# Local attention and Fourier mixing in one kernel: batch 0's three-point sums move to VectorE, crossbar transposes become 768 columns wide, and the planner counts eight DMA places

## The chip, the cores and the metric

The kernel runs on one core of a Trainium2 chip. The metric is the device time of one execution in microseconds (us), as a median over several runs. The core has TensorE (PE, with its weight loads PEld), VectorE (DVE), ScalarE (ACT), GpSimd (POOL) and SyncE (SP, which here only issues transfers). Sixteen DMA engines move the data.

## The reference

Four batches, eight heads, 768 positions, 64 numbers a head. First comes attention with a linear distance penalty, in which a query sees the 95 keys before it, itself, and the first eight keys of the sequence. Then follows a Fourier layer with a feed-forward block (model width 512, hidden width 2048).

```python
scores = scale * np.matmul(q, k.transpose(0, 1, 3, 2))
bias = -slopes[:, None, None] * dist[None, :, :]
scores = np.where(keep, scores + bias, -1e9)        # keep: local band or first 8 keys
x = np.matmul(softmax(scores), v)                   # heads side by side: (B, S, 512)
X = np.fft.fft(np.fft.fft(x, axis=1), axis=2)
u = x + np.real(X)
un = (u - mean(u)) / np.sqrt(var(u) + 1e-6)
out = u + np.maximum(un @ w_ch1, 0.0) @ w_ch2
```

## The kernel before, in words

**Attention.** For each batch and each pair of heads (hp 0 to 3), q and k are loaded as float32, cast to float16 (`cast_qk` L382 for batches 0 and 1, `cast_direct` L400 for 2 and 3) and transposed. Batches 0 and 1 use PE for that (`trans` L515, tile pt, copied out by DVE at L533 or ACT at L537). Batches 2 and 3 (`b >= FB`) use the DMA crossbar (`trans_dma` L499, issued by SP at L506): four transfers for each head pair, each of 64 partitions by 768 columns. `score` (L542) multiplies key tiles of 128 by the queries of the same and the next tile. In batches 0 and 1 the distance penalty is added by a further product; in batches 2 and 3 ACT's exponential goes to a buffer `er`, and DVE multiplies it with a mask `mk` (L592). `v_global` and `glob` treat the first eight keys, `av` (L665) multiplies with v and normalizes into X[b], and `bounce` (L720) writes X[b] to DRAM (xd) and reads it back in another order (xr), to be added later. Batch 0's bounce is issued by SP, the others' by ACT.

**Fourier layer.** The transform over 768 positions is split into a step of 6 and a step of 128, the one over 512 columns into a step of 4 and a step of 128. The small steps are sums on DVE, the large ones products on PE. For batches 1 to 3, `fold_s` (L741, stages f1 to f4) makes the two-point and three-point sums, and `fold_d` (L841, stages g1 and g2) the four-point sums over the columns. For batch 0 (`b < DB`, DB = 1), `fold_3` (L797) makes only the two-point and four-point sums; the three-point sum is left to PE, which adds three products with different tables in PSUM. `y_unit` (L878) makes these products, py: for batch 0 with tables t1 and t1x (five further blocks, 480 KB, loaded at L1290 into a buffer of the ring hT), for the others with t1 alone. `mirror` (L922) reverses parts on POOL, and `u_unit` (L961) makes the second product (pu), adds xr and normalizes.

**Feed-forward.** Each batch has three chunks of 256 rows, c = 0 to 11. `nt_unit` (L1052) transposes a chunk: on PE for c below 7 (ptu, copied out by DVE or ACT), and by two crossbar transfers of 128 by 512 from c = 7 (`nt_dma` L1043). `ph_unit` (L1081) makes the hidden layer, eight groups of eight products; `pg_unit` (L1104) and, from chunk 8, `pg_units` make the output. The weights come as eight transfers of 512 KB issued by POOL (L1345, L1350); their first one waits for POOL's cast of the last k of batch 1, whose staging shares their buffers. After the last one SP issues a small transfer (hold, L1359), and only behind this gate are the loads of batch 2 issued.

**Order.** The class `Plan` (L18) decides while the program is built in which order instructions stand. It keeps a clock for each engine, adds assumed costs, and picks the next step by time, then by a rank (a lower one first). `LAND` gives assumed landing times for the first transfers. Each engine runs its instructions in that fixed order, and SP and ACT issue their transfers in it too. A transfer issued by SP or ACT takes one of eight completion semaphores in turn, and it waits until the transfer that had this semaphore before it has landed; the plan before does not count that.

Of the kernel before, what the change touches and what calls it, by code (L numbers as in the profile page):

```python
# [14 lines left out]
P = 128  # L15


class Plan:  # L18
# [8 lines left out]
    LAND = {("xw", 0, 0): 36.0, ("xw", 0, 1): 37.6, ("xr", 0): 43.3, ("ld", 4, 2): 50.1, ("ld", 5, 2): 55.5, ("ld", 6, 2): 60.9,  # L27
            ("ld", 7, 2): 66.4, ("w1", 0): 45.8, ("w1", 1): 50.6, ("w1", 2): 54.3, ("w1", 3): 57.9, ("w2", 0): 61.6, ("w2", 1): 65.2, ("w2", 2): 68.1, ("w2", 3): 70.7}
    LAT = {"ACT": 0.14, "DVE": 0.12, "POOL": 0.08}

    def __init__(self):
        self.t = {"PE": 0.0, "ACT": 0.0, "DVE": 0.0, "POOL": 0.0, "SP": 0.7, "DMA": 1.9, "DMA2": 0.0}
        self.tok = {}
        self.ready = []
        self.pending = []
        self.rings = {}
        self.left = {}
        self.n = 0

# [23 lines left out]
    def later(self, ways, needs=(), after=0.0, outs=(), uses=(), ring=None, lat=0.0, dma=0.0, then=None, rank=1):  # L63

        self.n += 1
        self.pending.append((self.n, ways, list(needs), after, outs, uses, ring, lat, dma, then, rank))
        self.promote()
# [11 lines left out]
    def first(self):  # L79

        best = None
        for i, (ready, p) in enumerate(self.ready):
            c = (min(max(self.t[w[0]], r) for w, r in zip(p[1], ready)), p[10], ready[0], p[0], i)
            if best is None or c < best:
                best = c
        return best

    def emit(self, place):
        ready, (_, ways, needs, after, outs, uses, ring, lat, dma, then, _) = self.ready.pop(place)
# [12 lines left out]
        for u in uses:  # L102
            self.used(u, end + lat)
        if ring is not None:
# [5 lines left out]
    def pe(self, us, after=0.0):  # L110
# [6 lines left out]
    LOOK = 10  # L117

# [60 lines left out]
def kernel(  # L179
# [24 lines left out]
    DB = 1  # L204
# [78 lines left out]
    NBUF = {"hT": 3, "qk": 2, "qs": 3, "qkT": 4, "er": 2, "eg": 1, "x": 1, "xr": 1, "zy": 1, "eA": 1,  # L283
# [43 lines left out]
    def load(b, hp, which):  # L327
# [3 lines left out]
        if b >= FB:  # L331
            srcs = [(0, q), (1, k)] if which == "qk" else [(2, v)]
            for w, src in srcs:
                i = 1 + HP + 3 * (n - FB * HP) + w

                def run(src=src, i=i, w=w):
                    t = stage[("t", n, w)] = buf("qs", i, [P, 2 * NS, Dh], FP32, 1)
                    if w < 2:
# [5 lines left out]
                pl.later([("SP", 0.55 if w < 2 else 1.1, run)], free("qs", i) + gate, 0.0, [("ld", n, w)], lat=1.7, dma=2.67)  # L344
# [55 lines left out]
    def cast_direct(b, hp, w, i):  # L400
        n = HP * b + hp

        def cast(on):
            if n not in qk16:
                qk16[n] = buf("qk", n, [P, 2, 2, NP, 2, Dh], FP16, 1)
            for t in range(2):
                copy_on(on, qk16[n][:, t, w], stage[("t", n, w)].rearrange("p (h i t) d -> p t i h d", h=2, t=2)[:, t])
        pl.later([("ACT", act(768), lambda: cast("ACT")), ("POOL", 1.6, lambda: cast("POOL"))],
# [7 lines left out]
    def cast_v0(b, hp):  # L416
        n = HP * b + hp

        def cast():
            V0[n] = buf("er", n, [P, NP, 2, 2, Dh], FP16, 1)  # L420
            nc.gpsimd.tensor_copy(V0[n].rearrange("p n t h d -> p (n t) h d"),
                                  stage[("t", n, 2)].rearrange("p (h n) (t d) -> p h (n t) d", h=2, t=2).rearrange("p h j d -> p j h d"))
        pl.later([("POOL", 0.87, cast)], [("ld", n, 2)] + free("er", n), 0.0, [("vc", n)], [("free",) + vat(n)], rank=b)

    def v_place(b, hp):
        n = HP * b + hp

        def run(start, ring):
# [14 lines left out]
            pl.used(("free", "er", n), e)  # L443
# [43 lines left out]

    def kg_copies(b, hp):
        n = HP * b + hp
        for s in range(2):  # L490
            def cp(s=s):
# [3 lines left out]
                    TT[n][64 * s:64 * s + 64, 1, 0:P].rearrange("p (t m) -> p t m", t=2)[:, :, 0:NG // 2])  # L495
# [3 lines left out]
    def trans_dma(b, hp):  # L499
        n = HP * b + hp  # L500

        def xb(a, t):
            if n not in TT:
                TT[n] = buf("qkT", n, [P, 2, S], FP16, 6)
            o = TT[n].rearrange("p w (i a t m) -> p a t (w i) m", a=2, t=2, m=64)[:, a, t]
            nc.sync.dma_start_transpose(o, qk16[n][64 * a:64 * a + 64, t].rearrange("p w i h d -> p (w i h d)"))  # L506
        at = [(a, t) for a in range(2) for t in range(2)]
        for x, (a, t) in enumerate(at):
            pl.later([("SP", 1.3, lambda a=a, t=t: xb(a, t))],
                     ([("qk", n, 0), ("qk", n, 1)] + free("qkT", n)) if x == 0 else [("xb", n, x - 1)], 0.0,  # L510
                     [("xb", n, x)], lat=0.0, dma=0.01)
        pl.later([("SP", 0.0, lambda: None)], [("xb", n, 3)], 0.0, [("qkT", n)], [("free", "qk", n)], lat=2.2, dma=0.5)
# [28 lines left out]

    def score(b, hp, g):  # L542
        n = HP * b + hp
        idx = 2 * HP + 3 * (n - 2 * HP) + g

        def run(start, ring):
            pa = bank(ring, f"sc_{n}_{g}")
            w0, w1_ = ((256, CO), (CO, CO), (256, P))[g]
            tiles = ((2 * g, 0, w0), (2 * g + 1, 256, w1_))
            if b < 2:  # L550
# [10 lines left out]
            for i, c0, cw in tiles:  # L561
                for s in range(2):
                    lo = 64 * s
                    nc.tensor.matmul(pa[:, s, c0:c0 + cw], TT[n][lo:lo + 64, 1, i * P:(i + 1) * P],  # L564
                                     TT[n][lo:lo + 64, 0, i * P:i * P + cw], start=(b > 1), stop=True,
                                     skip_group_check=(b < 2))
            e = pl.pe(0.24 if b > 1 else 0.66, start)
# [17 lines left out]
            if b < 2:  # L585
# [17 lines left out]
        ATT.append(([("qkT", n)] + ([("sid", hp), ("c", "dist")] if b < 2 else []), BANKS(b), run))  # L603
# [29 lines left out]
    def glob(b, halves):  # L633
# [4 lines left out]
        def run(start, ring):  # L638
            pg = bank(ring, f"pgl_{b}_{halves[0]}")
            for half in halves:  # L640
                for i in range(2):
                    hp = 2 * half + i
                    nc.tensor.matmul(pg[32 * half:32 * half + 32, 0, :], kG[b % 2][:, hp, :],
                                     TT[HP * b + hp][:, 0, 256:S], start=(i == 0), stop=(i == 1),
                                     tile_position=(0, 32 * half))
            e = pl.pe(mm_us(512, 2 * len(halves)), start)
# [14 lines left out]
    XT = [("x", 0), ("hT", 4), ("x", 1), ("x", 2)]  # L661
# [3 lines left out]
    def av(b, part, jp):  # L665
# [8 lines left out]
        def run(start, ring):  # L674
# [31 lines left out]
            def norm():  # L706
                if b not in X:
                    X[b] = buf(XT[b][0], XT[b][1], [P, NS, Dm], FP16, 4 if b else 5)
# [11 lines left out]
    def bounce(b):  # L720
# [3 lines left out]
        for n, (c0, c1) in enumerate(parts):  # L724
            def wr(n=n, c0=c0, c1=c1):
# [3 lines left out]
                for t in range(2):  # L729
# [3 lines left out]
                     lat=1.7, dma=2.4 if b else 2.6)  # L733
# [6 lines left out]

    def fold_s(b):  # L741

        parts = ((0, 256), (256, 128), (384, 128)) if b == 0 else ((0, 512),)
# [732 lines left out]
```

## Time and profile before

| what | value |
|---|---|
| median of 9 runs | 269.54 us (269.02 to 271.84) |
| the profiled execution | 270.51 us, of which its span (first to last instruction) 268.7 us |
| instructions in the span | 6248, of which 2540 products on PE |
| granted clock of PE | 1.00 |
| moved by DMA | 42.03 MB, 75743 packets, 32834 of them under 512 bytes |
| HBM | 31.92 MB read, 9.44 MB written |

The page gives busy times of the engines, and the trace can be asked for groups of instructions, waits, the chain of work that ended last, and tables by stage. A product's listed length includes its way through the array, and products overlap; so what one costs in a row of many is read from the distance between starts. A wait is told with its releaser: `PE ph L1091 <- ACT hT L1097` means that PE stood idle before a ph product of line 1091 until ACT's instruction of line 1097 was done. SPq and ACTq are issues of transfers, in which the engine itself does nothing else.

### The profile page before, as it was taken

To read this page: it belongs to the slowest core of one execution; us is meant where nothing else is said; L and a number is where in the kernel's file an instruction comes from. 1 tells how busy PE (TensorE), PEld (TensorE's weight loads), DVE (VectorE), ACT (ScalarE), POOL (GpSimd) and SP (SyncE) were. 2 spreads that over 40 slices of the span, in tenths; PEclk is the share of its full clock that TensorE was granted. 3 is DMA by queue.
4 is the path that set the end of the run, shared out by engine and by line. 5 is a ranking of instruction groups with operands and counts; after the bars stand their busy time and mean duration, and the time that the engine had idled before them with its cause. 6 is when DMAs were issued, how large, how long until landed. Compare 5 with 4: busy or idle time off the path is not lost.

```text
span 268.7 us, 6248 instructions
## 1 busy us (share of the span) xinstructions
PE 255.0 (95%) x2540; PEld 181.2 (67%) x2540; DVE 171.8 (64%) x349; ACT 151.1 (56%) x263; POOL 61.0 (23%) x127
## 2 busy tenths in 40 slices
PE   7799899999999899999999799999999999999994
PEld 3454558577855776676675356759777668888883
DVE  4566873833399475861559957878998645525473
ACT  1479693987536737994891254896443345444300
POOL 1442298142010152321200307101100511010000
PEclk9999999999999999999999999999999999999999
DMA  7999969999689985997899896402072241311122
GB/s 211 290 294 307 280 158 256 217 215 213 130 157 255 279 161 133 207 192 130 209 156 174 181 315 150 106 2 41 0 168 109 59 92 47 81 40 41 39 82 78
DMA packets 75743, 42.03 MB, mean 156 GB/s; under 512 B 32834, under 2 KB 71746, under 8 KB 75714
## 3 DMA queue, kind: packets, MB, share of 16 engines
q1 hardware_dynamic: 68658, 32.71, 52.0%
q0 software_dynamic: 4224, 4.19, 9.5%
q10 hardware_dynamic: 2832, 4.72, 6.8%
q8 instruction: 20, 0.33, 0.5%
q14 instruction: 9, 0.07, 0.1%
HBM read 31.92 MB, written 9.44 MB: 154 GB/s over the span
## 4 chain that ended last, share of the span: by engine, by line
PE 66%; DMA 20%; DVE 5%; POOL 2%; SPq 2%; ACT 2%; issue 1%; ACTq 0%; POOLq 0%
PE ph L1091 26%; PE pg L1114 12%; DMA w<-in_moe_w_ch_dram 10%; DMA qs<-in_q_dram 5%; PE pgD L1195 5%; PE sc L564 4%; PE py L892 4%; PE pgA L1195 4%; PE pav L691 3%; DMA u<-in_v_dram 3%; PE pu L972 3%; DMA qs<-in_v_dram 2%; PE sc L559 2%; PE pt L527 1%; SPq L372 1%; POOL ww L940 1%
## 5 line engine op out<-in xcount | busy, mean ns | idle before, releaser
L1091 PE MATMUL ph<-unT,w 128*128 128x256 f16 x768 | 94.1, 273 | 2.7 <-ACT hT L1097 1.6
L1091 PEld LDWEIGHTS <-w 128*128 128x128 f16 x768 | 72.6, 98 | 17.1 <-issue 6.1
L1097 ACT ACTIVATE hT<-ph 128x512 f16<-128x512 f32 x78 | 46.2, 596 | 41.7 <-PE ph L1091 41.6
L1114 PE MATMUL pg<-w,hT 128*128 128x512 f16 x256 | 60.7, 379 | 0.0
L1114 PEld LDWEIGHTS <-hT 128*128 128x128 f16 x256 | 24.2, 98 | 23.4 <-issue 0.6
L587 ACT ACTIVATE ex<-sc 128x992 f16<-128x992 f32 (+2 forms) x24 | 20.8, 926 | 8.2 <-PE sc L564 8.2
L584 ACT ACTIVATE er<-sc 128x992 f16<-128x992 f32 (+2 forms) x24 | 21.6, 923 | 3.9 <-PE sc L564 3.1
L376 ACT ACTIVATE qk<-qs 128x384 f16<-128x384 f32 (+1 forms) x29 | 13.8, 526 | 15.1 <-DMA qs<-in_q_dram 5.1
L1098 DVE TENSOR_SCALAR hT<-ph 128x512 f16<-128x512 f32 x18 | 12.4, 691 | 11.6 <-PE ph L1091 11.6
L1123 DVE SCALAR_TENSOR_TENSOR u<-pg,sm,u 128x512 f32<-128x512 f32 x16 | 12.0, 748 | 12.1 <-PE pg L1114 12.1
L466 POOL CAST v<-qs 128x768 f16<-128x768 f32 x8 | 7.0, 879 | 52.6 <-DMA qs<-in_v_dram 52.6
L564 PE MATMUL sc<-qkT 64*128 64x256 f16 (+1 forms) x192 | 17.0, 262 | 1.4 <-ACT er L584 1.4
L691 PE MATMUL pav<-v,ex 128*128 128x65 f16 x352 | 16.3, 193 | 1.0 <-DVE x L711 0.7
L599 DVE TENSOR_TENSOR ex<-er,mk 128x992 f16<-128x992 f16 (+2 forms) x24 | 14.8, 624 | 3.6 <-ACT er L584 3.5
L691 PEld LDWEIGHTS <-ex 128*128 128x128 f16 x352 | 15.2, 97 | 2.4 <-DVE x L711 0.9
L564 PEld LDWEIGHTS <-qkT 64*128 64x128 f16 x192 | 5.9, 94 | 15.6 <-issue 14.0
L1038 POOL TENSOR_SCALAR sm<-sm 128x2 f32<-128x2 f32 x12 | 2.3, 193 | 57.1 <-ACT un L1031 57.0
L907 ACT ACTIVATE zy<-py 128x1024 f16<-128x1024 f32 (+1 forms) x12 | 10.0, 845 | 9.1 <-PE py L892 8.1
L940 POOL COPY ww<-zy 128x512 f16<-128x512 f16 x16 | 9.9, 650 | 22.9 <-PE py L892 20.8
L1031 ACT ACTIVATE un<-un 128x512 f16<-128x512 f16 x24 | 14.9, 624 | 0.3 <-PE ptu L1063 0.3
L991 DVE SCALAR_TENSOR_TENSOR u<-pu,xr 128x512 f32<-128x512 f32 x18 | 11.7, 688 | 5.0 <-PE pu L972 3.2
L1195 PEld LDWEIGHTS <-hT 128*128 128x128 f16 x128 | 12.5, 98 | 1.6
(129 smaller groups left out, 381.4 us busy)
## 6 DMA issues: line engine op xcount, KB each, us to landing
out_dram<-u SPq DMA_DIRECT2D x24, 256.0 KB, 2.4
w<-in_moe_w_ch_dram POOLq DMA_DIRECT2D x8, 512.0 KB, 19.4
qs<-in_q_dram SPq DMA_DIRECT2D x9, 384.0 KB, 6.1
qs<-in_k_dram SPq DMA_DIRECT2D x9, 384.0 KB, 6.5
qs<-in_v_dram SPq DMA_DIRECT2D x16, 192.0 KB, 4.7
xr<-xd ACTq DMA_DIRECT2D x3, 768.0 KB, 5.3
u<-in_v_dram SPq DMA_DIRECT2D x5, 384.0 KB, 7.1
w<-in_q_dram SPq DMA_DIRECT2D x4, 384.0 KB, 7.0
```

The costliest lines, as they stand in the source:

```text
L376: A(d, s, AF.Copy)
L564: nc.tensor.matmul(pa[:, s, c0:c0 + cw], TT[n][lo:lo + 64, 1, i * P:(i + 1) * P], TT[n][lo:lo + 64, 0, i * P:i * P + cw], start=(b > 1), s ...
L584: A(mine(), cut(pa), AF.Exp, 0.0, 0.125)
L587: A(cut(expst[hp][:, :, g * 512:g * 512 + (384 if g == 2 else 512)]), cut(pa), AF.Exp, 0.0, 0.125)
L599: VT(o, mine(), m, op=ALU.mult)
L691: nc.tensor.matmul(po[:, jj, hh * 65:(hh + 1) * 65], lhsT, v16[b % 2][:, i, h, 0:65], start=(jp == 0 and a == 0), stop=(a == len(ops) - 1) ...
L940: nc.gpsimd.tensor_copy(rev[:, n], T[("y", b)][:, n, :, :, ::-1])
L1031: A(x, x, AF.Square, accum_out=MV[c][:, a, 2:3])
L1091: nc.tensor.matmul(ph[:, a * CH:(a + 1) * CH], W1[0][:, d, jb * P:(jb + 1) * P], UNT[c][:, d, :], start=(d == 0), stop=(d == ND - 1))
L1097: pl.later([("ACT", act(512), lambda: A(dst, ph, AF.Relu)), ("DVE", dve(512), lambda: V.tensor_scalar_max(dst, ph, 0.0))], [], e, [("h", c ...
L1114: nc.tensor.matmul(pg, HT[c][:, jb, t * P:(t + 1) * P], W2[0][:, jb, :], start=(jb == 0), stop=(jb == NJ - 1))
L1195: nc.tensor.matmul(o, lhs(j), rhs(j), start=(first and j == 0), stop=(j == NK - 1), skip_group_check=True)
```

## The change

It has these parts:

1. DB goes from 1 to 0: batch 0 too uses `fold_s` and `fold_d`. Its columns are taken in two parts of 256, and these steps get rank -1 with a head start of 0.8 us in the plan. py of batch 0 has 24 products in place of 60, and t1x is not loaded.
2. `trans_dma` issues two transfers of 128 partitions by 768 columns for each head pair, one for q and one for k, each after its own cast. For that, k of batches 2 and 3 is loaded like v, in two transfers of 256-byte runs in place of one of 512-byte runs; and the products read q by strided patterns (`tile_of`).
3. Chunks from c = 3 on (before: from 7) are transposed by the crossbar, with one transfer of 128 by 1024. The layout of unT changes, so that a ph product reads two runs of 128 columns.
4. A whole cast of 768 columns replaces two of 384 in batches 2 and 3.
5. `cast_v0` gets buffers of its own (v0) in place of two of the ring er.
6. In batches 2 and 3 score products of 240 columns become 256 wide, and the products of `glob` go from one of 512 columns to two of 256.
7. The plan counts eight places for transfers, adds 0.1 us where PE goes between 64-row and 128-row products, and has other landing times.

```diff
-    LAND = {("xw", 0, 0): 36.0, ("xw", 0, 1): 37.6, ("xr", 0): 43.3, ...
+    LAND = {("xw", 0, 0): 34.3, ("xw", 0, 1): 36.3, ("xr", 0): 40.7, ...
...
+        self.lanes = [0.0] * 8
...
+            if p[11]:
+                ready = [max(r, self.lanes[p[11] - 1]) for r in ready]
+            c = (min(max(self.t[w[0]], r) for w, r in zip(p[1], ready)) - self.AHEAD * (p[10] < 0), p[10], ready[0], p[0], i)
...
+        for _ in range(nd):
+            self.lanes.append(max(end + lat, self.t[eng] + 2.2, *[self.LAND.get(o, 0.0) for o in outs]))
+            self.lanes.pop(0)
...
-    DB = 1
+    DB = 0
...
-                    if w < 2:
+                    if w < 1:
                         run_dma(t.rearrange("p (m t) d -> p m (t d)", t=2), src, b, h0)
                         return
...
+    def tile_of(n, lo, w, i, nb=1):
+
+        x = TT[n][lo:lo + 64, w]
+        if n < FB * HP or w:
+            return x[:, i * P:i * P + P].rearrange("p (t m) -> p t m", t=2)
+        if nb == 1:
+            return x.rearrange("p (i t a m) -> p i a t m", t=2, a=2, m=64)[:, i // 2, i % 2]
+        if i % 2 == 0:
+            return x.rearrange("p (i t a m) -> p i a t m", t=2, a=2, m=64)[:, i // 2]
+        o = (i // 2) * 256 + 64
+        return x[:, o:o + 384].rearrange("p (y q m) -> p y q m", y=2, m=64)[:, :, 0:3:2]
...
-        def xb(a, t):
+        def xb(w):
             if n not in TT:
                 TT[n] = buf("qkT", n, [P, 2, S], FP16, 6)
-            o = TT[n].rearrange("p w (i a t m) -> p a t (w i) m", a=2, t=2, m=64)[:, a, t]
-            nc.sync.dma_start_transpose(o, qk16[n][64 * a:64 * a + 64, t].rearrange("p w i h d -> p (w i h d)"))
...
+            nc.sync.dma_start_transpose(TT[n][:, w].rearrange("p (j x) -> p j x", x=P),
+                                        qk16[n][:, w].rearrange("p n t h d -> p (n t h d)"))
...
+    def RF(b):
+        return 1 if b else -1
...
-        parts = ((0, 256), (256, 128), (384, 128)) if b == 0 else ((0, 512),)
+        parts = ((0, 256), (256, 256)) if b == 0 else ((0, 512),)
...
-                nc.sync.dma_start_transpose(UNT[c][:, :, a * P:(a + 1) * P], T[("un", c)][:, a])
...
+            UNT[c] = buf("unT", c, [P, 2, ND, P], FP16, 1)
+            nc.sync.dma_start_transpose(UNT[c].rearrange("p a d m -> p (a d) m"), T[("un", c)].rearrange("p a f -> p (a f)"))
...
-        if c >= 7:
+        if c >= 3:
             return nt_dma(c)
...
-                    nc.tensor.matmul(ph[:, a * CH:(a + 1) * CH], W1[0][:, d, jb * P:(jb + 1) * P], UNT[c][:, d, :],
+                    nc.tensor.matmul(ph[:, a * CH:(a + 1) * CH].rearrange("p (x m) -> p x m", x=2), W1[0][:, d, jb * P:(jb + 1) * P], UNT[c][:, :, d, :],
...
-        def t1x_load():
-            T1X[0] = buf("hT", 3, [P, 5, 384], FP16, 4 * DB)
-            nc.sync.dma_start(T1X[0].rearrange("p a b -> p (a b)"), t1x_d.ap())
```

By the instruction order of the changed kernel, batch 0's ten sums of the first part stand on DVE right behind the third normalization of head pairs 0 and 1, and the ten of the second part behind its last normalization. On PE all four transpositions of batch 1 now stand ahead of batch 0's py; before, three did. Three of the four copies out of these transpositions are on ACT (before: one).

## The prediction

> **What bounds the kernel now.** I read the shares of the engines first, then five stages of the span, then TensorE's own waits, the chain of work, the SP queue, and last the groups of instructions that the change removes.
>
> ```profile
> PE 255.0 (95%) x2540; PEld 181.2 (67%) x2540; DVE 171.8 (64%) x349; ACT 151.1 (56%) x263; POOL 61.0 (23%) x127
> ```
> ```profile
> 0.00:54.00 54.00, 48.43 (x572) 28.80 (x573) 33.77 (x85) 35.67 (x51) 23.18 (x50) 1.00 1.04 252
> 54.00:83.00 29.00, 28.43 (x327) 20.88 (x327) 15.53 (x30) 19.36 (x42) 6.90 (x11) 1.00 0.96 181
> 83.00:165.00 82.00, 78.74 (x711) 52.97 (x708) 53.98 (x103) 49.13 (x88) 18.96 (x41) 1.00 0.92 198
> 165.00:250.00 85.00, 84.62 (x807) 66.00 (x804) 59.59 (x119) 45.08 (x81) 11.99 (x26) 1.00 0.26 67
> ```
>
> The first number after a stage is its length, then come the busy times of PE, PEld, DVE, ACT and POOL, the granted clock, the DMA share and GB/s. TensorE is busy 95% of the span, at full clock. From 54 us on it is hardly ever idle, and from 165 us not at all. So an instruction taken from PE after 54 us shortens the span by its own time, unless PE then waits. The DMA engines are the other loaded part: about full up to 165 us, idle after.
>
> ```profile
> PE ph L1091 <- ACT hT L1097: 1.6, 1, 1.6
> PE sc L564 <- ACT er L584: 1.4, 1, 1.4
> PE ph L1091 <- ACT ex L587: 1.1, 1, 1.1
> PE pu L972 <- POOL ww L940: 0.4, 1, 0.4
> ```
>
> These are PE's waits from 53 us on (total, times, longest). By the timeline they sit at 86.7, 152.8, 53.1 and 211.5 us. In the first two ACT stands in its own queue: at 85.5 to 88.0 it casts a late load and makes masks before the hidden-layer copy, and from 146.8 to 152.1 it waits to issue the xr read.
>
> ```profile
> 37.96 3.53 PE py L892 x32
> 41.48 1.43 POOL w L1350 x2
> 42.91 27.80 DMA w<-in_moe_w_ch_dram
> 71.14 0.39 SPq L372
> 101.89 0.45 PE ptu L1063 x8
> ```
> ```profile
> 29.13 1.21 SPq L1290 DMA_DIRECT2D hT<-t1xm  x1
> 30.44 3.50 SPq L730 DMA_DIRECT2D xd<-x  x4
> ```
>
> Start, length, what. The front is a race of PE with the weight transfer: batch 0's first DFT product (py), then 27.8 us of weights, whose end lets the loads of batch 2 start at 71.1. Ahead of them the SP queue issues the second table t1x, and the x write stands behind it.
>
> **Part 1, PE work removed.** Batch 0's py has 60 products of 128x256; by the timeline they run from 37.89 to 44.45 us, 0.109 us each. With the three-point sums done beforehand it has 8+8+6+2 = 24, as the instruction order of the changed kernel confirms: 36 x 0.109 = 3.9 us off. Chunks 3 to 6 leave PE's transpose: 4 x 0.45 us (the ptu piece above) = 1.8 us off, with four evacuations of 0.69 us on DVE or 1.01 us on ACT. Added: 48 score products go from 240 to 256 columns, in pairs that run together, 24 x 16 columns at 2.4 columns a ns (256 in 0.109 us with its overhead) = 0.2 us. Blocks of 64-row score products between 128-row work go from 44 to 46; entering and leaving such a block costs 0.2 to 0.3 us in the starts of the trace, so 0.5 us. Net 3.9 + 1.8 - 0.7 = 5.0 us.
>
> **Part 2, moving operand in two runs.** Hidden-layer products (768 of them) now read two runs of 128 columns. The nearest row is L554, whose operand is 240 columns twice: 366 ns for 480 columns, while one run of 496 takes 375. The 9 ns are the 16 columns. Cost 0; the upper end is one or two ns each, 1.5 us.
>
> **Part 3, the front.** Sums on DVE, a part of 256 columns, by distances between starts: two 768-element sums 0.94, two of 512 0.68, two of 256 0.40, two scalings 0.28, two scalar-tensor operations 0.66: 3.0 us a part, 6.0 for both. The old folds took 2.4 there (24.37 to 25.3 and 31.53 to 33.02), and the last stage stays near 4. So DVE gains 3.5 us of work. The first part fills gaps (1.3 us between 25.3 and 27.7) and puts off x by about 0.6, to 32.1. Then 3.0 of sums and 1.9 of the first four-point stage: py can start at 37.0. PE reaches it at 38.7 (37.9 now, plus one 0.78 us transposition that is moved ahead), so the sums are covered by 1.7 us; if that cover goes, each us shows. The dearer move is on ACT: three copies of the transposed q and k (1.35 us apart) stand in its queue before y instead of one, and ACT was already 90% busy from 30 to 40 us. From the last q load at 31.1: two casts to 31.95, three copies 4.05, six exponentials 5.0, gives 41.0; the y copies and one exponential between them end at 43.6. So the first pu starts at 43.6, not 44.45, but PE has by then done a transposition and a score group more. From there 7.1 us of PE remain before ph, not 8.6 plus the 1.1 stall: ph starts at 51, not 54.4.
>
> t1x is gone: 480 KB at 290 GB/s of that stretch is 1.65 us, and everything behind it on the SP queue and the rings (x write, xr read, v of batch 1) moves up by that. The first weight issue waits for POOL's last cast; the k load lands at 34.4, a 0.9 us cast and the issue follow at 35.5 instead of 37.4. So weights, gate and loads of batch 2 come 1.7 to 1.9 us earlier. PE now runs ahead of its data: v of head pair 2, 60.95 now, lands at about 59, is ready at 60.0, and PE would be there at 58.2, a stall of 1.7. After it 54.4 to 83.3 is the same work: chunk 2's ph starts at about 81.1. The front gives 2.2 us of the 3.9 + 1.1 (between 1.0, if ACT is later, and 3.3, without the stall).
>
> **Part 4, crossbar and loads.** The SP queue had 32 transposes for q and k and 10 for the chunks, all at least 1.2 us. Now 16 and 9. No row shows 128x768 or 128x1024; but 64x768 (96 KB) and 128x512 (128 KB) both take 1.2 us of SP and land after 2.4 us alone, so I take 1.2 and 2.9; if it went by bytes, 1.8 to 2.4 and up to 4.8. Even so SP does not get busier. The Trainium skill, "VectorE: DVE Perf Modes", "The three transpose paths", says the crossbar needs 1309 ns for a 128x128 block, TensorE 390, and its rules prefer TensorE. By it eight blocks in a row are an estimated 10.5 us of latency a chunk, and the move would be a loss wherever ph follows at once. In this trace four blocks land after 2.4 us, and PE has two to four us of pg work between u and ph of these chunks. I take the row: the move costs PE nothing. Behind each transpose on SP stand the next load and the stores; they have slack of several us.
>
> k of batches 2 and 3 is now read in 256-byte packets. In the packet records a packet takes 28 ns at 512 bytes (q, k at 72 us) and 27.6 at 256 (v at 75 us), so a k load goes from 1.3 to 2.6 us of all 16 engines: 8 x 1.3 = 10.5 us. Four more chunks cross the DMA, 4 x 1.3 = 5. This falls in 83 to 165 us, at share 0.92 where the front reached 1.04. Casts: 28 of ACT's half casts (0.46 apart) become 9 whole ones (0.75) and 7 on POOL: ACT 6 us lighter, POOL 3 us heavier, with room.
>
> **Part 5, stalls from 83 us on:** 1.6 + 1.4 + 0.4 and two of 0.2 = 3.8 us. In the changed order all masks stand ahead of chunk 2's copies, two copies stand between the xd write and the xr read, and batch 2's scores begin some 20 us of PE work earlier. I count 2.6 of the 3.8 as gone; the order has new waits on k casts. Ends: 0 and 3.8.
>
> Sum: front -2.2, transposes -1.8, scores and blocks +0.7, stalls -2.6: -5.9. The profiled execution (270.51, span 268.7) becomes about 264.6 with a span of 262.8. The median of the runs, 269.54, lies 1.0 below the profiled one: 263.7.
>
> **The rivals.** *Stalls stay* (chance 0.22): the removed PE time comes through, but ACT's queue waits at other loads and none of the 3.8 is recovered: 269.5 - 2.2 - 1.8 + 0.7 = 266.2. For it: the order is fixed beforehand and loads land up to 6 us apart. Against: attention is placed earlier against its use. *Everything fits* (0.16): front 3.3, all stalls gone: 269.5 - 3.3 - 1.8 + 0.7 - 3.8 = 261.3. *DMA becomes the bound* (0.09), slower: the stage from 83 to 165 us now moves 0.92 x 82 = 75 us of transfer and gets 15.5 more, 91. If the 16 engines sustain a share of 1.00, batches 2 and 3 get their data 9 us late, PE waits at their scores, and the time is 263.7 + 9 = 272.7; at 1.04, the share of the front, 6 us late, the gain is just gone, and above that the kernel is faster. Against: until about 150 us PE has feed-forward work of batches 0 and 1, and after 165 us, where the share is 0.26, lateness can be made up. That batch 0's sums would not be ahead is excluded by the order.
>
> **Numbers.** The main case has 0.53 (262.3 to 265.3). Range 261.0 to 268.0: reaching from near the best case past the stalls-stay case, leaving out the DMA case and the far ends. A measurement can tell about 0.5%, 1.3 us. Faster 0.86, within 0.05, slower 0.09.
>
> **What will show it.** 2480 products; 24 of py for batch 0, starting at 38.5 to 39.5; ph near 51; the first load after the gate near 69.3; chunk 2's ph near 81; the waits of 1.6 and 1.4 gone; transposes of about 1.2 us each on SP. I am wrong if 768 ph products take more than 0.109 us each, if py waits for DVE, or if scores of batch 2 wait for qkT.

## The result, and the profile after

The changed kernel takes 272.84 us (median of 17 runs, 271.05 to 279.44), the kernel before 269.76 on the same chips: ratio 1.0101, 95% interval 1.0079 to 1.0123. It is slower by 1%, where 263.7 us was forecast. The profiled execution took 272.94 us, with a span of 271.2. Executions more than 1.5% above the fastest of the same kernel are left out of this and every later ratio.

The page's row of busy times, and the same four stages as before (length, busy PE, PEld, DVE, ACT, POOL, granted clock, DMA share, GB/s):

```profile
PE 254.7 (94%) x2480; PEld 179.1 (66%) x2480; DVE 172.4 (64%) x359; ACT 148.1 (55%) x247; POOL 63.2 (23%) x130
```
```profile
0.00:54.00 54.00, 48.59 (x556) 27.96 (x556) 39.00 (x103) 38.96 (x59) 24.00 (x52) 0.97 1.05 247
54.00:83.00 29.00, 28.11 (x327) 20.73 (x316) 15.60 (x30) 18.24 (x36) 7.61 (x11) 1.00 1.00 185
83.00:165.00 82.00, 75.96 (x693) 52.64 (x691) 52.78 (x107) 46.17 (x76) 24.07 (x50) 0.98 1.09 206
165.00:250.00 85.00, 85.00 (x771) 63.13 (x771) 55.33 (x107) 41.76 (x75) 7.48 (x17) 1.00 0.23 63
```

60 of the 2540 products are gone, and yet PE's busy time fell by only 0.3 us, in the main because two stretches ran at half clock; a later run of the same instructions without such stretches has PE busy for 251.3 us. The loss lies behind 83 us, for the most part in one stage. From 83 to 165 us PE is busy 2.8 us less than before (idle for 6.0 us, before 3.3), while the DMA share rose from 0.92 to 1.09. By the starts of the products, chunk 2's ph begins at 82.33 us (before: 83.31), 1.0 us early; chunk 9's begins at 221.00 (before: 218.74), 2.3 us late.

PE's waits from 54 us on, in the changed kernel:

```profile
PE sc L599 <- DMA qkT<-qk: 2.4, 1, 2.4
PE ph L1136 <- ACT hT L1142: 1.7, 3, 0.8
PE sc L599 <- ACT er L621: 1.5, 2, 1.3
PE pvp L453 <- POOL v L437: 0.9, 1, 0.9
```

The old waits (1.6, 1.4, 1.1) have gone, but larger ones stand in their place, and the first is new in kind: scores waiting for a transpose. The chain of work shows what lies ahead of that one (start, length, what), and the transposes as a group show their duration on SP and their landing:

```profile
128.21 5.24 DMA qkT<-qk
133.47 8.63 DMA qkT<-qk
```
```profile
L533 SPq DMA_TRANSPOSE qkT<-qk x16: 1210/1609/3758, 76.8 to 154.0; - x16
DMA to landing us min/median/max: 3.0/4.9/8.6
```

A transpose of 128x768 takes 1.2 us of SP at best, as forecast; in its place here it takes 1.6 in the median, and the one that PE waits for at 139.7 us needs 8.6 us to land, while loads and x's stores are under way.

### The profile page after: what moved, and what is told of

Read it like the earlier page. It is cut to its first block, busy times and chain, and to the rows that moved or that the text cites. A ratio compares the mean times of both kernels' runs of the same rounds, so it can differ in the third digit from the quotient of the medians.

```text
span 271.2 us, 6101 instructions
## 1 busy us (share of the span) xinstructions
PE 254.7 (94%) x2480; PEld 179.1 (66%) x2480; DVE 172.4 (64%) x359; ACT 148.1 (55%) x247; POOL 63.2 (23%) x130
## 4 chain that ended last, share of the span: by engine, by line
PE 59%; DMA 13%; DVE 11%; ACT 6%; SPq 6%; issue 2%; POOL 0%; ACTq 0%; DVEq 0%
PE ph L1136 25%; PE pg L1159 14%; DMA qkT<-qk 5%; DMA qs<-in_q_dram 5%; PE pgD L1240 5%; SPq L388 4%; PE pgA L1240 4%; DMA w<-in_q_dram 3%; PE pu L1019 3%; PE pav L735 3%; PE py L939 2%; PE sc L599 2%; ACT er L621 2%; ACT ex L624 1%; ACT qk L392 1%
## 5 line engine op out<-in xcount | busy, mean ns | idle before, releaser
L1142 ACT ACTIVATE hT<-ph 128x512 f16<-128x512 f32 x83 | 49.2, 596 | 55.1 <-PE ph L1136 48.6
L735 PE MATMUL pav<-v,ex 128*128 128x65 f16 x352 | 17.2, 196 | 1.1 <-ACT ex L624 1.0
L735 PEld LDWEIGHTS <-ex 128*128 128x128 f16 x352 | 16.0, 100 | 2.6 <-issue 1.6
L1143 DVE TENSOR_SCALAR hT<-ph 128x512 f16<-128x512 f32 x13 | 9.0, 689 | 12.4 <-PE ph L1136 12.3
L1085 POOL TENSOR_SCALAR sm<-sm 128x2 f32<-128x2 f32 x12 | 2.9, 240 | 57.7 <-ACT un L1078 53.8
L396 POOL CAST qk<-qs 128x768 f16<-128x768 f32 x8 | 7.5, 935 | 28.9 <-DMA qs<-in_k_dram 19.7
L755 DVE TENSOR_TENSOR x<-pav,rc 128x512 f16<-128x512 f32 (+1 forms) x21 | 12.9, 615 | 0.7
L1258 DVE SCALAR_TENSOR_TENSOR u<-pgA,sm,u 128x256 f32<-128x256 f32 (+1 forms) x12 | 6.9, 572 | 9.9 <-PE pgA L1240 9.5
L392 ACT ACTIVATE qk<-qs 128x768 f16<-128x768 f32 x10 | 8.4, 842 | 8.1 <-DMA qs<-in_q_dram 5.7
```

What stands on the lines that cost most here:

```text
L735: nc.tensor.matmul(po[:, jj, hh * 65:(hh + 1) * 65], lhsT, v16[b % 2][:, i, h, 0:65], start=(jp == 0 and a == 0), stop=(a == len(ops) - 1) ...
L755: VT(X[b][:, 2 * jp:2 * jp + 2, first * Dh:(first + nh) * Dh].rearrange("p j (h d) -> p j h d", d=Dh), pv[:, :, :, 0:Dh], rc.to_broadcast( ...
L1142: pl.later([("ACT", act(512), lambda: A(dst, ph, AF.Relu)), ("DVE", dve(512), lambda: V.tensor_scalar_max(dst, ph, 0.0))], [], e, [("h", c ...
```

## The experiments

Three theories stood at the start. **Theory 1**: the DMA engines are full from 83 to 145 us, because k comes in 256-byte packets and four more chunks cross them, so the data is late. **Theory 2**: the order in which the planner now puts the work is what costs, whatever the transfers. **Theory 3**: the two stretches at half clock cost 1.7 us each. Theories 4 and 5 were formed after the first eight runs.

Since the order is fixed while the program is built, edits are of two kinds: those that leave every instruction in its place, and those that let the planner order anew.

### Same order, one thing taken away

*k in 512-byte runs.* In batches 2 and 3 k is read in another row order, so that part of the computation differs.

```diff
+                    if w == 1:
+                        tk = t.rearrange("p (m t) d -> p m (t d)", t=2)
+                        xk = src[b, h0:h0 + 2].rearrange("h s d -> (h s) d").rearrange("(m p t) d -> p m (t d)", p=P, t=2)
+                        for t2 in range(2):
+                            nc.sync.dma_start(tk[64 * t2:64 * t2 + 64], xk[64 * t2:64 * t2 + 64])
+                        return
```

> The changed kernel with one edit: the k of batches 2 and 3 is read in runs of 512 bytes in place of 256, still two transfers a head pair, so that k's rows land in another order (this part of the computation is changed); every instruction stands where it stood. Theory 1 (the DMA engines are full from 83 to 145 us, and the fixed order makes TensorE wait for what they bring late): 8 loads lose about 1.3 us each, 10.5 us of 16 engines' time, the share from 83 to 165 us falls from 1.09 to about 0.95, the 2.4 us wait of the scores at 139 us and the slow clock after it (1.7 us) go, and with the other stalls that grew there the time is 266 to 268.5 us. Theory 2 (the waits come from the new order of work on ScalarE and VectorE): 272 to 273 us. Theory 3 (the two dips of the granted clock are what was lost): the second dip goes with its wait, the first stays, about 270 us.

Measured: ratio 1.0037 (1.0004 to 1.0071) against 1.0101, so 1.7 us less than the change. The stage and the wait of the scores:

```profile
83.00:165.00 82.00, 75.53 (x703) 52.56 (x701) 52.91 (x107) 47.40 (x77) 24.07 (x50) 1.00 1.04 204
```
```profile
PE sc L605 <- DMA qkT<-qk: 2.6, 1, 2.6
```

The share fell to 1.04, where 0.95 was expected, and the wait of the scores stayed at 2.6 us. Theory 1 carries part of the loss and not the rest.

*No idle array.* Zeros are multiplied in the two long waits.

```diff
+            if (b, first, jp) == (0, 4, 0):
+                for _ in range(18):
+                    nc.tensor.matmul(po[:, 1, 0:P], EG[:, 0:P], EG[:, 0:P], start=True, stop=True)
...
+            if (n, g) == (12, 0):
+                for _ in range(42):
+                    nc.tensor.matmul(pa[:, 0, 0:P], EG[:, 0:P], EG[:, 0:P], start=True, stop=True)
```

> The changed kernel in its own order, with multiplications of zeros put into its two long waits: 18 of 128 columns ahead of the products at 25.5 us, 42 ahead of the scores at 139 us. They end about when the data comes. Theory 3 (the dips of the granted clock after these waits cost 1.7 us each): no dip at 27.5 and 143.6 us, 270 to 271.5 us. If the dips cost nothing because other waits follow: 272 to 273.5 us.

Measured: ratio 1.0106 (1.0071 to 1.0141); the clock stayed at 1.00 in the profile. Nothing is gained, so theory 3 falls as a cause of the loss. Three of the changed kernel's own executions also kept a mean clock of 1.00, and took 271.9, 272.9 and 273.7 us.

### Parts of the change alone

Here the planner orders anew. First, batch 0's sums with the eight places, and all else as before; then the same with chunks 3 to 6 on the crossbar:

```diff
-        if c >= 3:
+        if c >= 7:
             return nt_dma(c)
...
-        for w in range(2):
-            pl.later([("SP", 1.3, lambda w=w: xb(w))], ...
+        at = [(a, t) for a in range(2) for t in range(2)]
+        for x, (a, t) in enumerate(at):
+            pl.later([("SP", 1.3, lambda a=a, t=t: xb(a, t))], ...
```

> Batch 0's sums on VectorE and the order with eight DMA places alone; the loads, the casts, the q and k transposes (four of 64x768 a head pair) and chunks 3 to 6 on TensorE are as before the change. Theory 1: the DMA load is that of before, TensorE has 3.9 us less work, some of it lost to the front: 265 to 267.5 us. Theory 2: the order is what costs, so no gain: 269 to 273 us. Theory 3: 1.7 us are lost wherever a wait of over about 1.4 us stands ahead of a dip; one dip near 27 us as in the changed kernel.

> As the run with the sums alone, but with chunks 3 to 6 transposed by the crossbar as in the changed kernel, in one transfer a chunk. Theory 1: 1.8 us less on TensorE than with the sums alone, 5 us more on the DMA engines, whose share from 83 to 165 us stays near 0.98: 264 to 267 us. If already these transfers are too much: 268 to 270 us. Theory 2: 269 to 273 us.

Measured: 1.0090 (1.0065 to 1.0114) and 1.0003 (0.9983 to 1.0023). With 3.8 us less PE work the first is slower than before, as theory 2 has it; the chunks' transfers then help by 2.3 us instead of hurting. The next run is the whole change with chunks 3 to 6 back on PE (the first hunk above alone):

> The changed kernel with chunks 3 to 6 transposed on TensorE again, as before the change. Theory 1: TensorE gets 1.8 us more work, the DMA engines about 5 us less (4 transposes of 1.3 us) between 83 and 145 us, so about half of what the transfers cost comes back: 269.5 to 272 us. Theory 2: the added work comes on top, 274 to 275 us. Theory 3: the first dip stays as the front is the same; the second may go with its wait.

Measured: 1.0305 (1.0233 to 1.0377). Fewer transfers, 5.5 us slower than the change: theories 1 and 2 missed, theory 2 by less, and theory 3 had given no time. Then the kernel before with one part each: the eight places, the chunks, and the 768-column transfers with k's load, casts and `tile_of`; the core of each edit:

```diff
+            if p[11]:
+                ready = [max(r, self.lanes[p[11] - 1]) for r in ready]
```

> The kernel before, with the eight DMA places in its planner and nothing else of the change. Theory 1: work and DMA load are those of before, so 269 to 270.5 us. Theory 2: the new order alone costs what the sums should have brought, 271 to 273 us.

```diff
-        if c >= 7:
+        if c >= 3:
```

> The kernel before, with chunks 3 to 6 transposed by the crossbar too (two transfers of 128x512 a chunk, as chunks 7 to 11 have them) and nothing else of the change. What the two runs with and without these chunks gave beside the sums, a ratio of 1.0003 against 1.0090, is 2.3 us; if it holds here, 267 to 268 us. If theory 1 held for these transfers (8 of 1.2 us, some 5 us of the 16 engines), 269.5 to 271 us.

```diff
-                    if w < 2:
+                    if w < 1:
...
-            nc.sync.dma_start_transpose(o, qk16[n][64 * a:64 * a + 64, t].rearrange("p w i h d -> p (w i h d)"))
+            nc.sync.dma_start_transpose(TT[n][:, w].rearrange("p (j x) -> p j x", x=P),
+                                        qk16[n][:, w].rearrange("p n t h d -> p (n t h d)"))
```

> The kernel before, with the 768-column crossbar transfers of q and k alone: k in 256-byte runs, casts by parts, two transfers a head pair, the scores' strided operand. Theory 1: 10.5 us more DMA work between 70 and 150 us, where the share was 0.92, so stalls of the scores: 271.5 to 274 us. Theory 2: the transfers cost nothing without the new order (they take 1.2 us of SP in place of 4.8): 268.5 to 270.5 us.

Measured: 1.0201 (1.0127 to 1.0276), 1.0318 (1.0252 to 1.0383), and for the last 280.0 us, the mean of two of its four executions, 278.8 and 281.2 (the 283 us in a later expectation is the median of all four), against 269.96. Each of the three alone costs 2 to 4%, though none adds more than 0.3 us of PE work. Not run alone were the new landing times, the 0.1 us between 64- and 128-row products, and the buffers v0; the runs with the sums have them all. The opposite edit, the changed kernel planned without places:

```diff
-        if nd is None:
-            nd = int(dma > 0 and ways[0][0] in ("SP", "ACT"))
+        nd = 0
```

> The changed kernel with the eight DMA places taken out of the planner (every operation takes zero places), so that only the order of the work differs. If the order that the places bring is what costs (theory 2), 268 to 270.5 us. If the DMA engines' load costs under any order (theory 1), 271 to 275 us, with scores waiting for transfers again.

Measured: 1.0122 (1.0049 to 1.0194), the change's own loss. The places are not what costs in this order; they hardly shape it, as the plan ends at the same time, 258.6 us, without them.

### How lateness reaches PE: ScalarE's queue

The worst kernel shows the way. ScalarE in the run with the 768-column transfers alone (start, busy, what; in brackets the idle time before it and what ended it):

```profile
91.01 0.84 ACT L376 ACTIVATE qk<-qs 128x768 f16<-128x768 f32 x1 [5.77 <-DMA qs<-in_k_dram]
91.76 1.07 ACT L1120 ACTIVATE hT<-ph 128x512 f16<-128x512 f32 x2
92.71 1.51 ACT L930 ACTIVATE zy<-py 128x1024 f16<-128x1024 f32 x2
103.41 0.84 ACT L376 ACTIVATE qk<-qs 128x768 f16<-128x768 f32 x1 [9.19 <-DMA qs<-in_q_dram]
104.16 1.01 ACT L930 ACTIVATE zy<-py 128x1024 f16<-128x1024 f32 x1
```

ScalarE runs in order. At 94.2 us it comes to a cast whose load of q lands 9.2 us later, and the copy of y behind it, whose products were done at 98.4 us, stands too. Before that a cast of k, 5.8 us late, held up the copies of the hidden layer in the same way. PE, in the same kernel, waits 4.8 us for those copies and 4.2 for that of y:

```profile
PE ph L1114 <- ACT hT L1120: 4.8, 1, 4.8
PE sc L578 <- ACT zy L930: 4.2, 1, 4.2
```

In the changed kernel it is the same at 104 us, with a smaller wait; the exponential behind the cast is what the scores then wait for:

```profile
104.02 0.84 ACT L392 ACTIVATE qk<-qs 128x768 f16<-128x768 f32 x1 [2.64 <-DMA qs<-in_q_dram]
104.77 0.79 ACT L621 ACTIVATE er<-sc 128x768 f16<-128x768 f32 x1
```

This is **theory 4**. The test keeps the order and moves the casts to GpSimd:

```diff
-        pl.later([("ACT", act(768), lambda: cast("ACT")), ("POOL", 0.87, lambda: cast("POOL"))],
+        pl.later([("ACT", act(768), lambda: cast("POOL")), ("POOL", 0.87, lambda: cast("POOL"))],
```

> The changed kernel in its own order, with one edit: the nine casts of q and k that ScalarE does between 73 and 153 us (843 ns each) are done by GpSimd at the same places of the order. Theory 4 (late loads reach TensorE through ScalarE's queue: a cast that waits for a load holds up the exponentials and evictions behind it): the wait of the scores for an exponential at 104 us (1.3 us) and those for hidden units at 85 to 120 us (1.7 us) shrink, 269.5 to 271.5 us. Theory 1 (the transfers themselves are late): the wait at 139 us for a transpose stays, 272 to 273.5 us. GpSimd's own queue may hold up the sums behind the casts: to 274 us.

Measured: 1.0049 (1.0006 to 1.0091), but this rests on six of 14 executions. All 14 scatter from 268.8 to 278.8 us, with a median of 273.5 (the changed kernel: 272.8), so a gain is not shown. In the profiled execution (271.06 us) PE's waits from 54 us on have changed as theory 4 has it:

```profile
PE sc L599 <- DMA qkT<-qk: 2.3, 1, 2.3
PE pu L1019 <- POOL rev L975: 1.8, 2, 0.9
PE ph L1136 <- ACT hT L1142: 0.3, 1, 0.3
```

The wait for the exponential is gone and that for hidden units is 0.3 in place of 1.7 us; GpSimd's queue takes back 1.8, and the wait for the transpose stays. The same edit in the run with sums and chunks:

> The run with the sums and the chunks (64x768 transposes), in its own order, with all casts of q and k of batches 2 and 3 on GpSimd. Theory 4: ScalarE's 8 to 10 us of waiting for loads and for the transposes' buffer between 80 and 180 us goes; 266 to 268.5 us. If ScalarE's queue held up nothing there: 269 to 270.5 us.

Measured: 1.0004 (0.9968 to 1.0040) after 1.0003. Nothing is gained there. So the profiles show that lateness passes through ScalarE's queue, and no run shows that taking the casts out of it saves time.

### Why the data is late: the plan's costs

The planner's clock can be printed as the program is built. For head pair 12 (the first of batch 3) it says, beside the profile, in us:

| kernel | transposes landed: plan | profile | first score: plan | profile |
|---|---|---|---|---|
| before | 147.5 | 147.7 | 148.0 | 150.7 |
| changed | 134.1 | 142.1 | 135.1 | 142.2 |

Before, plan and chip agree on the data within 0.2 us. The change plans it 13 us earlier and gets it 8 us after the plan. The planner charges the two-transfer load of k 2.67 us, as it did the single one, and each transpose 0.5; for q it charges only 2.0, where the plan before charged 2.67. The transfers of a head pair come to 8.34 us in all (before: 8.55), though they have become dearer. It also seems to expect no gain: its PE clock ends at 258.6 us, before at 258.3. But 5.0 us of that are the 0.1 us that it adds at each of 50 changes between 64- and 128-row products, for which the plan before charges nothing. **Theory 5**: the order is made for transfers that are faster than real ones, so it puts batches 2 and 3 ahead of feed-forward work that could have covered them. Test: the changed kernel with other costs in the planner only.

```diff
-... lat=1.7, dma=2.0 if w < 1 else 2.67, nd=1 + (w > 0))
+... lat=1.7, dma=(2.0, 3.4, 2.67)[w], nd=1 + (w > 0))
...
-                     [("xb", n, w)], lat=1.9, dma=0.5)
+                     [("xb", n, w)], lat=1.9, dma=1.0)
...
-                 lat=2.2, dma=0.6)
+                 lat=2.2, dma=1.0)
```

> The changed kernel with higher transfer costs in its planner alone: k 3.4 us in place of 2.67, a q or k transpose 1.0 in place of 0.5, a chunk's transpose 1.0 in place of 0.6; with these its plan has the k loads of batch 3 land at 122 to 155 us, where the profile of the changed kernel has them at 117 to 153 us and its plan at 114 to 145 us. Theory 5 (the plan believes the new transfers to be faster than they are, so the order asks TensorE, ScalarE and SP for data that comes 4 to 8 us later): the lag behind the plan falls from 8.4 us to 4 to 5 us, 267.5 to 270 us. Theory 2 (each new order is a draw, whatever its costs): anywhere from 270 to 278 us. Theory 1 (load alone): 272 to 274 us.

Measured: 266.7 us, ratio 0.9896 (0.9850 to 0.9942). The lag behind the plan at the last head pair is 1.7 us. The transfers are the same ones, in the same stage, and PE's waits from 54 us on have shrunk to four:

```profile
83.00:165.00 82.00, 80.95 (x720) 53.62 (x718) 56.67 (x111) 45.58 (x72) 25.71 (x48) 1.00 1.10 212
```
```profile
PE pvp L453 <- POOL v L437: 1.8, 1, 1.8
PE pu L1019 <- POOL ww L987: 0.5, 1, 0.5
PE pav L724 <- DVE x L755: 0.3, 1, 0.3
PE pu L1019 <- POOL rev L976: 0.2, 1, 0.2
```

PE is busy 80.95 of 82 us at a DMA share of 1.10, a little above the 1.09 at which the changed kernel idled. So the load by itself is not the bound: theory 1 is refuted as the main cause. The loads of k for batches 2 and 3 now land 0.6 to 4.3 us ahead of the plan, except the last (2.4 behind). So the raised cost is not truer for k alone. In the changed kernel a load of k takes 5.2 us in the median from its first issue to landing, where the plan counts 5.5, and it lands late because it is issued late; it is a load of q (5.7, planned 4.3) and a transpose (4.9, planned 3.7) that take longer than planned. The raised costs work as a margin. Chunk 5's last ph is at 139.4 us (changed: 149.0, before: 139.0), and the first score of head pair 12 at 152.6, 13 us after its transposes. To tell costs from luck, intermediate costs, k's cost alone, and the gaining version again:

```diff
-... lat=1.7, dma=(2.0, 3.4, 2.67)[w], nd=1 + (w > 0))
+... lat=1.7, dma=(2.0, 3.1, 2.67)[w], nd=1 + (w > 0))
...
-                     [("xb", n, w)], lat=1.9, dma=1.0)
+                     [("xb", n, w)], lat=1.9, dma=0.8)
...
-                 lat=2.2, dma=1.0)
+                 lat=2.2, dma=0.8)
```

> The changed kernel with transfer costs of the planner about half-way between those of the change and those of the raised run: k 3.1 us, a q or k transpose 0.8, a chunk's transpose 0.8; its plan has the k loads of batches 2 and 3 land up to 7 us later than the change's. Theory 5 (too low costs are what costs time): between the two, 267 to 271 us. Theory 2 (each order a draw): 270 to 278 us, no relation to the costs.

```diff
-... lat=1.7, dma=2.0 if w < 1 else 2.67, nd=1 + (w > 0))
+... lat=1.7, dma=(2.0, 3.4, 2.67)[w], nd=1 + (w > 0))
```

> The changed kernel with only the planner's cost of a k load raised, 2.67 to 3.4 us; the transposes' costs are those of the change. Theory 5: most of the lag came from the loads, 267.5 to 270.5 us; if the transposes' costs carry it, 271 to 273 us. Theory 2: 270 to 278 us.

> The changed kernel with the raised costs once more, in five rounds, for a firmer interval: 266 to 268 us, ratio 0.986 to 0.993.

Measured: 0.9970 (0.9950 to 0.9991), 1.0026 (1.0001 to 1.0051), 0.9888 (0.9852 to 0.9924). Next come the worst kernel with k 3.4 and transposes 1.0, the kernel before with one cost raised, and the changed kernel with costs that are too high:

```diff
-... [("ld", n, w)], lat=1.7, dma=2.0 if w < 1 else 2.67)
+... [("ld", n, w)], lat=1.7, dma=(2.0, 3.4, 2.67)[w])
...
-                     [("xb", n, w)], lat=1.9, dma=0.5)
+                     [("xb", n, w)], lat=1.9, dma=1.0)
```

> The kernel before with the 768-column transfers alone, which took 283 us, with the planner's costs raised as in the run that gained: k 3.4 us in place of 2.67, a q or k transpose 1.0 in place of 0.5. Theory 5: the load of q at which ScalarE stood 9.2 us and the two waits of 4 to 5 us at 87 and 101 us go, 268 to 273 us. Theory 2: no help, 272 to 284 us. Theory 1: 280 us or more, as the transfers are the same.

```diff
-        pl.later([("SP", 0.0, lambda: None)], [("xb", n, 3)], 0.0, [("qkT", n)], [("free", "qk", n)], lat=2.2, dma=0.5)
+        pl.later([("SP", 0.0, lambda: None)], [("xb", n, 3)], 0.0, [("qkT", n)], [("free", "qk", n)], lat=2.2, dma=1.0)
```

> The kernel before with one cost of its planner raised, 0.5 to 1.0 us for the transposes of a head pair; its plan ends at 259.8 us in place of 258.3, with 2.2 us of idle TensorE after 80 us in place of 0.7. Theory 5: its loads landed on the plan already, so raised costs bring nothing: 269.5 to 273 us. If raised costs help any order: 266 to 269 us.

```diff
-... lat=1.7, dma=(2.0, 3.4, 2.67)[w], nd=1 + (w > 0))
+... lat=1.7, dma=(2.0, 3.6, 3.0)[w], nd=1 + (w > 0))
...
-                     [("xb", n, w)], lat=1.9, dma=1.0)
+                     [("xb", n, w)], lat=1.9, dma=1.2)
...
-                 lat=2.2, dma=1.0)
+                 lat=2.2, dma=1.2)
```

> The changed kernel with transfer costs above what its profile shows: k 3.6, v 3.0, transposes 1.2 us; its plan ends at 265.1 us with 8.1 us of idle TensorE after 80 us, where the gaining run's ends at 258.4 with 0.4. Theory 5: the order now holds work back for data that is there, and the planned loss of 6.7 us comes on top of 266.7 us, less a lag of 1 to 2 us that goes: 270 to 274 us. If only higher is better: 266 us or less.

Measured: 1.0096 (1.0066 to 1.0126), some 8 us less than the same kernel with the low costs; 1.0003 (0.9982 to 1.0024); 1.0170 (1.0126 to 1.0214). Raising a cost helps the two kernels that were planned too fast; in the kernel before it does not, and too high a cost loses what the plan says. Single values (270.2 and 274.1 us) lie in theory 2's wide range too; what speaks for theory 5 is the sequence. In the changed kernel, from its own costs through k's alone and half-way to the raised ones, each step is faster than the last, the repeat agrees, and too high costs are slower again. Lag is how far the first score of the last head pair starts behind the plan; plan, lag and span are in us, of the profiled execution. A star marks plans without the 0.1 us charge:

| kernel | plan's PE end | lag | span | ratio |
|---|---|---|---|---|
| before * | 258.3 | 5.4 | 268.7 | 1 |
| before, cost raised * | 259.8 | 4.2 | 268.1 | 1.0003 |
| changed | 258.6 | 8.4 | 271.2 | 1.0101 |
| k's cost alone | 258.4 | 6.3 | 269.3 | 1.0026 |
| half-way | 258.6 | 3.2 | 266.4 | 0.9970 |
| raised | 258.4 | 1.7 | 264.7 | 0.9896 |
| too high | 265.1 | 3.7 | 272.7 | 1.0170 |
| 768 columns alone * | 258.6 | 16.1 | 279.4 | - |
| the same, raised * | 258.6 | 7.5 | 271.3 | 1.0096 |
| sums alone | 260.5 | 4.4 | 271.0 | 1.0090 |
| sums and chunks | 258.7 | 3.7 | 266.9 | 1.0003 |
| places alone * | 261.1 | 9.5 | 275.7 | 1.0201 |
| chunks alone * | 269.1 | 4.1 | 277.8 | 1.0318 |
| chunks back on PE | 261.1 | 8.9 | 276.0 | 1.0305 |
| changed, no places | 258.6 | 7.3 | 270.1 | 1.0122 |

In every row plan plus lag is 3.9 to 6.1 us below the span: what follows the last head pair runs nearly as planned. The table says where time is lost, not why: lag is all that PE has fallen behind by then, through late data or otherwise. Rows with a star compare only among themselves. The order of the kernel before has 46 of those changes, 41 of them ahead of the last head pair; charged afterwards, its plan would end near 262.9 us and its lag be about 1.3, an estimate. So on equal terms the change's plan was some 4 us better, the kernel before kept close to its plan, and the changed one did not.

The table also tells the single parts apart. The chunks alone lose in the plan itself (269.1), the 768-column transfers through lag, the places by both. The rest of theory 2 stays true in this form: a new order is drawn at every edit. What settles its time is the plan's end and how far PE falls behind it. The kernel with the chunks back on PE lags by 8.9 us; its two largest waits, 3.2 and 2.7 us, are for exponentials on ScalarE, and what made those late was not followed further.

## Why the prediction was wrong

**Part 1 held** in its counts: 60 products fewer, by their columns 3.8 us less of py, 1.7 less of ptu and 0.2 more of scores. PE's busy time in the run with raised costs, which has the same instructions at full clock, is 3.7 us below the 255.0 of before; 5.0 was summed.

```profile
PE 251.3 (95%) x2480; PEld 176.4 (67%) x2480; DVE 175.6 (66%) x362; ACT 145.1 (55%) x243; POOL 66.2 (25%) x131
```

**Part 2 held**: the distance between starts of ph products is 109 ns in both kernels.

**Part 3 was mis-sized.** Chunk 2's ph starts at 82.3 us, forecast 81.1: the front gave 1.0 of 2.2 us. py starts at 39.5 (38.7 forecast) and waits 0.8 us for a copy on ScalarE; ph starts at 52.8 (51 forecast); products with v wait 1.0 us at 25.9 for exponentials. The stall for v at 60 us is there (0.9, forecast 1.7), and the loads behind the gate start at 69.7 (69.3).

**Part 4 failed**, at "they have slack of several us". The price of a transpose was right (1.2 us of SP and 3.0 us to land at best, for six blocks in a row as for a chunk's eight: the row and not the rule that was set against it), and so was the volume: 91 us were forecast for 83 to 165 us, and 1.09 x 82 is 89. But slack is what a fixed order leaves, and this order was made with lower charges for dearer transfers. At their places a transpose landed after 4.9 us in the median, where the forecast had 2.9. From the second on, the loads of k for batches 2 and 3 land 2 to 8 us behind the plan (before: at most 1.1, but for the last, 4.1), and ScalarE, SP and PE stand at the places that the plan gave them.

**Part 5 failed**, at "I count 2.6 of the 3.8 as gone". From 83 us on PE's waits sum to 6.0 us, where 3.8 stood before and 1.2 were left in the forecast. The placing of attention some 20 us earlier was counted as help against stalls, but the data did not come as much earlier. The first scores of batch 2 start 12.4 us sooner (93.8, before 106.2), while the k loads of its first three head pairs land within 0.8 us of where they did before. The new waits on casts, named and not priced, came. So did a sign of being wrong that was named, scores waiting for qkT, though in batch 3.

With costs raised, the steps from 83 us on come out: 264.74 - 82.66 = 182.1 us from chunk 2's ph to the end, before 268.73 - 83.31 = 185.4, so 3.3 us gained where 3.7 was forecast. In the changed kernel it is 271.15 - 82.33 = 188.8 us, 3.4 lost. Behind the front the change was worth about what was summed, and its plan lost it. Over the whole kernel the run with raised costs gains 3.0 us of the 5.9 forecast, as its front gives 0.7 in place of 2.2.

**The rival** *DMA becomes the bound* named 272.7 us, and came within 0.2, in part by luck. Its mechanism holds in part only: data is late and the scores wait. But it took a share of 1.00 to 1.04 for the limit of the engines, and the raised run sustains 1.10 without those waits. The limit was the order.

## What to carry to other kernels

Where a program's order is planned from assumed costs, an edit must be judged with its plan: print when the plan believes each load to land, set the profile's landing times beside it, and try other costs before judging the edit. Here three constants made the difference between 1.0% slower and 1.1% faster, at the same instructions' work and the same transfers, and costs a step higher lost 1.7%. An instruction that waits for a transfer holds up all that stands behind it on its engine; what brought time here was to plan it later, and moving it to another engine was not shown to.

## What the runs showed of the hardware

The granted clock fell to one half for 3.4 us after waits of PE, twice in the changed kernel's profile (apart from its last 1.3 us, when PE has no more work), never in the one of before. The 3.4 us ahead of each dip, and the dip:

```profile
24.10:27.50 3.40, 1.95 (x18) 0.86 (x19) 3.30 (x12) 3.40 (x5) 1.07 (x1) 1.00 1.12 325
27.50:30.90 3.40, 3.27 (x43) 3.18 (x43) 2.08 (x5) 2.11 (x5) 0.05 (x1) 0.50 1.14 322
140.20:143.60 3.40, 1.45 (x16) 1.11 (x17) 1.22 (x3) 1.64 (x3) 1.29 (x4) 1.00 0.85 184
143.60:147.00 3.40, 3.33 (x18) 2.23 (x16) 3.04 (x7) 2.52 (x4) 0.22 (x2) 0.50 1.06 302
```

The waits ahead of them were 1.0 and 0.4 us (25.9 to 27.6), and 2.4 us (from 139.7). The Trainium skill, "TensorE: Matmul & The Clock Gate", "HAM oscillation — how this bites in real kernels", warns of idle gaps above about 3.4 us; here shorter ones were enough, while a wait of 3.2 us in the run with the chunks back on PE left no dip, nor did a stretch of that run in which PE was busy for only 1.38 us:

```profile
149.80:153.20 3.40, 1.38 (x11) 1.05 (x11) 1.18 (x3) 2.73 (x5) 0.00 (x0) 1.00 1.35 199
```

What decides was not settled. Filling the two waits kept the clock up and changed the time by nothing that can be measured.

The 16 DMA engines showed a share of 1.31 from 83 to 100 us in the changed kernel, where 1.04 had been taken for their limit:

```profile
83.00:100.00 17.00, 15.94 (x154) 12.29 (x153) 13.05 (x28) 9.71 (x15) 5.67 (x12) 1.00 1.31 253
```

A share above 1 also says that this figure counts times that overlap, so it is no percentage of a limit.
